# One load of x, turned into columns on VectorE, and a separate buffer for the output rows, in a one-token decoder block

## The chip, the cores and the metric

The kernel runs on one core of a Trainium2 chip. The metric is the device time of the whole kernel in microseconds (us), taken as the median of several executions. An execution counts as slow when it takes over 1.5% longer than the fastest of its kernel.

Engine names in the profile: PE is TensorE's matmuls, PEld its weight loads, DVE is VectorE, ACT is ScalarE, POOL is GpSimd, SP is SyncE. A q behind the name (SPq, ACTq) is the engine's instruction queue, from which DMAs are issued. L143 is line 143 of the kernel. A line number of a helper can stand for many calls.

## The reference

One token passes through an attention layer with a cache of 65,536 positions, then through a gated feed-forward layer. Both have a layer norm before and a residual after.

```python
x = A_x                                   # [1, 1, 1024], bf16
# attention: 32 query heads, 4 kv heads, head size 128
q = layernorm(x) @ wq                     # wq [1024, 4096]
p = softmax(q @ k_cache.T / sqrt(128))    # k_cache, v_cache [1, 4, 65536, 128]
h = x + (p @ v_cache) @ wo                # wo [4096, 1024]
# feed-forward
n = layernorm(h)
out = h + (gelu(n @ w_gate) * (n @ w_up)) @ w_down   # 1024 <-> 3584
```

Everything is read once. The inputs are 173 MB, nearly all of it cache and weights; x and the output are 2 KB each.

## The kernel before

All large tensors pass through one pool of five buffers of 128 x 16384 bf16 (4 MB each). SyncE issues their loads in program order, each as soon as its buffer is free. The first two hold wq, the next three the first parts of k.

x was loaded twice by ScalarE: as columns (128 partitions, 8 elements each) for the layer norm, and as four rows of 256 for the residual, which TensorE adds to the output rows in PSUM.

```python
x_row = lead.tile([4, D // 4], BF16, name="x_row")
x_pc_bf = lead.tile([P, DC], BF16, name="x_pc_bf")          # P = 128, DC = 8
# ...
nc.scalar.dma_start(out=x_pc_bf[:], in_=A_x[0, 0].rearrange("(p c) -> p c", c=DC))
nc.scalar.dma_start(out=x_row[:], in_=A_x[0, 0].rearrange("(g n) -> g n", g=4))
for c0 in range(0, DC, WB):
    wv = load(wq_v[:, c0:c0 + WB, :], "wq_sb")             # two loads of 4 MB on SyncE
# ...
nc.vector.tensor_copy(out=x_pc[:], in_=x_pc_bf[:])
layernorm_cols(x_pc[:], xn_bf[:], "ln1")
# ... xnz (xn in padded columns), q = xn @ wq, k transposes, scores, softmax, values, wo ...
for g in range(4):                                         # the residual
    out_mm(ident_bf[0:4, g:g + 32], lambda g: x_row[:], False, False, groups=[g])
# ... feed-forward, the last matmuls add w_down's product into f_ps ...
o_fin = rows.tile([P, OW], BF16, name="o_fin")             # pool that reuses earlier space
nc.vector.tensor_copy(out=o_fin[0:97, :], in_=f_ps[0:97, :])
nc.sync.dma_start(out=out[0, 0].rearrange("(g n) -> g n", n=OW), in_=o_fin[0:97:32, :])
```

Of the kernel before, what the change touches and what calls it, by code (L numbers as in the profile page):

```python
# [11 lines left out]
BF16 = mybir.dt.bfloat16  # L12
# [5 lines left out]
def kernel(  # L18
# [13 lines left out]
    nc = tc.nc  # L32
    P = 128
    D = A_x.shape[-1]
    Hkv, Sk, Dh = A_k_cache.shape[1], A_k_cache.shape[2], A_k_cache.shape[3]
    HD = A_wq.shape[1]
    Hq = HD // Dh
    rep = Hq // Hkv
    F = B_w_gate.shape[1]
    DC = D // P  # L40
# [19 lines left out]
    lead = ctx.enter_context(tc.tile_pool(name="lead", bufs=1))  # L60
# [3 lines left out]
    sel = lead.tile([P, 32], F32, name="sel")  # L64
    hmask = lead.tile([P, rep], F32, name="hmask")
    x_pc = lead.tile([P, DC], F32, name="x_pc")
    x_row = lead.tile([4, D // 4], BF16, name="x_row")
    ident_bf = lead.tile([P, P], BF16, name="ident_bf")
    x_pc_bf = lead.tile([P, DC], BF16, name="x_pc_bf")
    xn_bf = lead.tile([P, DC], BF16, name="xn_bf")  # L70
    neg_half = lead.tile([P, 1], F32, name="neg_half")
    oT_all = lead.tile([P, Hq], BF16, name="oT_all")
    used = sum(-(-b // 32) * 32 for b in (4 * P, 4 * P, 2 * (W0 + NS * P), 128, 4 * rep, 4 * DC, D // 2, 2 * P,
                                          2 * DC, 2 * DC, 4, 2 * Hq))
    lead.tile([P, (-(used + 128)) % 4096], mybir.dt.uint8, name="lead_pad")
    chpool = ctx.enter_context(tc.tile_pool(name="chpool", bufs=NBUF))
    const = ctx.enter_context(tc.tile_pool(name="const", bufs=1))
    small = ctx.enter_context(tc.tile_pool(name="small", bufs=2))
    ps_m = ctx.enter_context(tc.tile_pool(name="ps_m", bufs=1, space=PSUM))
    actx = ExitStack()  # L80
    qkpool = actx.enter_context(tc.tile_pool(name="qkpool", bufs=2))
# [58 lines left out]
    def mm(out, lhsT, rhs, start, stop, loaded=False, tile_position=None, skip_group_check=False):  # L140
        t = nc.tensor
        if not loaded:
            return pe(t.matmul(out, lhsT=lhsT, rhs=rhs, start=start, stop=stop, tile_position=tile_position,  # L143
                               skip_group_check=skip_group_check))
        op = t.add_instruction(mybir.InstMatmult(  # L145
            name=nc.get_next_instruction_name(), engine=t.engine, start_tensor_calc=start, stop_tensor_calc=stop,
            tile_size=(lhsT.shape[0], lhsT.shape[1]), tile_position=tile_position or (0, 0), ldweights=False,
            bass_skip_group_check=skip_group_check,
            ins=[t.lower_ap(rhs), t.lower_ap(lhsT, for_matmul_weights=True)], outs=[t.lower_ap(out, opt=True)]))
        reuses.add(op.ins.name)  # L150
        return pe(op)
# [11 lines left out]
    wq_v = A_wq.rearrange("(p c) n -> p c n", c=DC)  # L163
    WB = max(1, CW // HD)
    assert HD <= CW and DC % WB == 0
    nc.scalar.dma_start(out=x_pc_bf[:], in_=A_x[0, 0].rearrange("(p c) -> p c", c=DC))
    nc.scalar.dma_start(out=x_row[:], in_=A_x[0, 0].rearrange("(g n) -> g n", g=4))
    wq_tiles = []
    for c0 in range(0, DC, WB):
        wv = load(wq_v[:, c0:c0 + WB, :], "wq_sb")  # L170
# [15 lines left out]
    for bp in range(4):  # L186
        s0 = 64 * (bp // 2) + bp % 2
        nc.vector.tensor_copy(out=esel[:, bp, :, :],
                              in_=ident_bf[:, s0:s0 + 63:2].unsqueeze(1).to_broadcast([P, 4, 32]))

    def layernorm_cols(src_col, dst_bf, tagp):
        s1 = small.tile([P, 1], F32, name=f"{tagp}_s1", tag="ln_s1")
        nc.vector.tensor_reduce(out=s1[:], in_=src_col, axis=AX.X, op=ALU.add)  # L193
        tot = ps_m.tile([P, 1], F32, name=f"{tagp}_tot", tag="misc")
        mm(tot[:], ones_f[:], s1[:], True, True)
        mean = small.tile([P, 1], F32, name=f"{tagp}_mean", tag="ln_mean")
        nc.vector.tensor_scalar(out=mean[:], in0=tot[:], scalar1=1.0 / D, scalar2=None, op0=ALU.mult)
        xc = small.tile([P, DC], F32, name=f"{tagp}_xc", tag="ln_xc")
        nc.vector.tensor_scalar(out=xc[:], in0=src_col, scalar1=mean[:, 0:1], scalar2=None, op0=ALU.subtract)
        sq = small.tile([P, DC], F32, name=f"{tagp}_sq", tag="ln_sq")  # L200
        s2 = small.tile([P, 1], F32, name=f"{tagp}_s2", tag="ln_s2")
        nc.vector.tensor_tensor(out=sq[:], in0=xc[:], in1=xc[:], op=ALU.mult)
        nc.vector.tensor_reduce(out=s2[:], in_=sq[:], axis=AX.X, op=ALU.add)
        tot2 = ps_m.tile([P, 1], F32, name=f"{tagp}_tot2", tag="misc")
        mm(tot2[:], ones_f[:], s2[:], True, True)
        ve = small.tile([P, 1], F32, name=f"{tagp}_ve", tag="ln_ve")
        nc.vector.tensor_scalar(out=ve[:], in0=tot2[:], scalar1=1.0 / D, scalar2=eps, op0=ALU.mult, op1=ALU.add)
        rstd = small.tile([P, 1], F32, name=f"{tagp}_rstd", tag="ln_rstd")
        nc.gpsimd.tensor_tensor(out=rstd[:], in0=ve[:], in1=neg_half[:], op=ALU.pow)
        nc.vector.tensor_scalar(out=dst_bf, in0=xc[:], scalar1=rstd[:, 0:1], scalar2=None, op0=ALU.mult)  # L210

    nc.vector.tensor_copy(out=x_pc[:], in_=x_pc_bf[:])  # L212
    layernorm_cols(x_pc[:], xn_bf[:], "ln1")

    def padded(pool, vec, ncols, name, tag=None):
# [192 lines left out]
    rows = ctx.enter_context(tc.tile_pool(name="rows", bufs=1))  # L408
# [19 lines left out]
    for wc in range(Hq // WN):  # L428
        wv = load(wo_v[:, wc * WN:(wc + 1) * WN, :], "wo_sb")
        for cc in range(WN):  # L430
            c = wc * WN + cc
# [4 lines left out]
    OW = D // 4  # L436
    f_ps = ps_f.tile([P, OW], F32, name="f_ps")

    def out_mm(stat, mov, first, last, groups=range(4)):
        for g in groups:  # L440
            mm(f_ps[32 * g:32 * g + 32, :], stat, mov(g), first, last, tile_position=(0, 32 * g),
               skip_group_check=True)
# [1 line left out]
    assert OW == 32 * DC  # L444
    out_mm(ones_f[:, 0:32], lambda g: at_r[:, g // 2, g % 2 * OW:g % 2 * OW + OW], True, False)
    for g in range(4):
        out_mm(ident_bf[0:4, g:g + 32], lambda g: x_row[:], False, False, groups=[g])
    h_t = rows.tile([P, DC, 32], F32, name="h_t")
    nc.vector.transpose(out=h_t[:].rearrange("p c j -> p (c j)"), in_=f_ps[:].rearrange("p (i c) -> p c i", c=DC))
    hn_bf = const.tile([P, DC], BF16, name="hn_bf")  # L450
# [66 lines left out]
    for sz in sizes:  # L517
        wv = load(wd_v[:, c0:c0 + sz, :], "wd_sb")
        for cc in range(sz):
            c = c0 + cc  # L520
            out_mm(actz[:, c, :], lambda g: wv[:, cc, g * OW:(g + 1) * OW], False, c + 1 == FC)
        c0 += sz
    o_fin = rows.tile([P, OW], BF16, name="o_fin")
    nc.vector.tensor_copy(out=o_fin[0:97, :], in_=f_ps[0:97, :])
    nc.sync.dma_start(out=out[0, 0].rearrange("(g n) -> g n", n=OW), in_=o_fin[0:97:32, :])

# [29 lines left out]
```

## Time and profile before

| | before |
|---|---|
| time at first, median of 3 | 408.83 us |
| span of the profiled execution | 407.1 us |
| busy: PE, DVE, ACT | 73%, 50%, 11% |
| moved by DMA | 173.19 MB, 425 GB/s over the span |

The page of the kernel before cuts the span into 40 slices of 10.2 us. A digit of the DMA row is the busy share of the 16 DMA engines in tenths, 9 standing for 90% or more; the row below it is the rate.

```profile
DMA  9999999999999999999999999999999999999995
GB/s 374 451 412 444 430 425 451 410 451 425 427 448 415 454 417 441 435 412 454 422 443 431 422 445 422 440 435 425 441 422 443 431 422 451 417 432 437 434 416 214
q10 hardware_dynamic: 152, 0.00, 0.0%
```

The DMA engines are busy from the first slice to the last but one. PE is idle for a quarter of the span, and no compute engine is near its limit over the whole span. The Trainium skill, "HBM Reference", section "Specifications (TRN2)", says that a core streaming alone measures about 425 GB/s, bounded by its 16 DMA engines. This trace agrees: 425 GB/s over the span. The third line is the queue of ScalarE: 152 packets, those of the two loads of x and their completions.

The issues of the kernel before (tensor, issuing queue, count, KB each, median us from issue to landing):

```profile
k_sb<-in_A_k_cache_dram SPq DMA_DIRECT2D x16, 4096.0 KB, 32.5
x_pc_bf<-in_A_x_dram ACTq DMA_DIRECT2D x1, 2.0 KB, 13.7
```

A 4 MB tile takes about 10 us to move at this rate but lands 32.5 us after its issue: two to three tiles are waiting ahead of it. That is the reserve of the load stream. The 2 KB of x take 13.7 us.

The timeline of the kernel before at the start and at the end (start, duration, engine, line, operation, count; in brackets the idle time before it and what ended it):

```profile
14.56 0.17 DVE L212 CAST x_pc<-x_pc_bf 128x8 f32<-128x8 bf16 x1 [13.49 <-DMA x_pc_bf<-in_A_x_dram]
18.48 0.18 DVE L218 COPY xnz<-xn_bf 128x8 bf16<-128x8 bf16 x1
25.14 0.69 DVE L229 COPY q_ev<-q_ps 128x512 f32<-128x512 f32 x1 [6.47 <-PE q_ps L145]
31.51 8.89 DVE L272 STREAM_TRANSPOSE k_sb<-k_sb 128x2048 uint32<-128x2048 uint32 x4 [3.74 <-DMA k_sb<-in_A_k_cache_dram]
402.97 1.04 PE L143 MATMUL f_ps<-wd_sb,actz 128*32 128x256 bf16 x12 [0.20 <-DMA wd_sb<-in_B_w_down_dram]
404.06 0.42 DVE L524 CAST o_fin<-f_ps 97x256 bf16<-97x256 f32 x1 [11.85 <-PE f_ps L143]
404.57 0.65 SPq L525 DMA_DIRECT2D out_dram<-o_fin  x1
```

Everything at the start waits for x until 14.56 us, q is ready for eviction at 25.14, but the next user, the first transpose of k, waits for its own load until 31.51. At the end the last weights release the last matmuls at 402.97, then come the cast and the output DMA.

### The profile page before, as it was taken

How to read it: one execution, taken by the hardware profiler on the slowest of the kernel's cores; microseconds unless marked ns; L12 is line 12 of the kernel's file. 1: busy time of each engine (PE TensorE's matmuls, PEld its weight loads, DVE VectorE, ACT ScalarE, POOL GpSimd, SP SyncE). 2: the span in 40 equal slices, each digit the busy share in tenths (PEclk: the TensorE clock that was granted, in tenths of full speed). 3: DMA queues.
4: the chain of work that ended last, by engine and by line, in shares of the span. 5: the costliest groups of instructions: out<-in, count | busy, mean ns of one | idle time of the engine just before them, and what ended most of it. 6: DMA issues, size and time to landing. Idle time of an engine off the chain costs nothing.

```text
span 407.1 us, 2657 instructions
## 1 busy us (share of the span) xinstructions
PE 298.8 (73%) x1481; PEld 64.1 (16%) x713; DVE 202.0 (50%) x183; ACT 44.9 (11%) x67; POOL 7.4 (2%) x17
## 2 busy tenths in 40 slices
PE   0266286879996789799966969998767997714464
PEld 0111011111110111211101111110102111300233
DVE  0218989966573678546464878181853001110110
ACT  1010001050000041000000420000051001000000
POOL 2000000000000000000000000000010000100000
PEclk9996879889999969699978798999887899767865
DMA  9999999999999999999999999999999999999995
GB/s 374 451 412 444 430 425 451 410 451 425 427 448 415 454 417 441 435 412 454 422 443 431 422 445 422 440 435 425 441 422 443 431 422 451 417 432 437 434 416 214
DMA packets 6652, 173.19 MB, mean 425 GB/s; under 512 B 872, under 2 KB 880, under 8 KB 1136
## 3 DMA queue, kind: packets, MB, share of 16 engines
q1 hardware_dynamic: 6488, 173.02, 98.7%
q8 instruction: 8, 0.13, 0.1%
q10 hardware_dynamic: 152, 0.00, 0.0%
q14 instruction: 4, 0.03, 0.0%
HBM read 173.02 MB, written 0.00 MB: 425 GB/s over the span
## 4 chain that ended last, share of the span: by engine, by line
DMA 46%; PE 30%; DVE 18%; ACT 4%; issue 1%; SPq 0%; ACTq 0%; DVEq 0%
DMA k_sb<-in_A_k_cache_dram 32%; DVE k_sb L272 12%; PE acc_ps L145 12%; DMA wg_sb<-in_B_w_gate_dram 9%; PE qk_ps L143 6%; PE qk_ps L145 6%; DMA wd_sb<-in_B_w_down_dram 5%; PE acc_ps L143 4%; DVE mx L293 3%; ACT sc L292 2%; DVE pT L317 1%; ACT pe_r L314 1%; PE o_ps L143 1%; DVE acc_sb L343 1%; ACT acc_sb L345 1%
## 5 line engine op out<-in xcount | busy, mean ns | idle before, releaser
L272 DVE STREAM_TRANSPOSE k_sb<-k_sb 128x2048 uint32<-128x2048 uint32 x64 | 142.1, 2278 | 31.6 <-DMA k_sb<-in_A_k_cache_dram 31.6
L143 PE MATMUL qk_ps<-k_sb,wsel 128*128 128x512 bf16 x256 | 103.7, 405 | 34.7 <-DVE k_sb L272 21.3
L145 PE MATMUL acc_ps<-v_sb,pT 128*128 128x512 bf16 x384 | 114.3, 410 | 0.0
L145 PE MATMUL qk_ps<-k_sb,wsel 128*128 128x512 bf16 x256 | 103.2, 403 | 0.0
L143 PE MATMUL acc_ps<-v_sb,pT 128*128 128x512 bf16 x128 | 52.9, 413 | 0.0
L143 PEld LDWEIGHTS <-wsel 128*128 128x128 bf16 x256 | 26.0, 101 | 138.3 <-issue 118.2
L293 DVE TENSOR_REDUCE mx<-qk_ps 128x1 f32<-128x1024 f32 x16 | 19.5, 1220 | 45.8 <-ACT sc L292 45.7
L292 ACT COPY sc<-qk_ps 128x1024 f32<-128x1024 f32 x16 | 16.2, 1012 | 201.8 <-PE qk_ps L145 201.7
L143 PEld LDWEIGHTS <-pT 128*128 128x128 bf16 x128 | 13.8, 108 | 101.9 <-issue 101.9
L317 DVE STREAM_TRANSPOSE pT<-pe_r 128x1024 bf16<-128x1024 bf16 x16 | 19.0, 1227 | 6.2 <-ACT pe_r L314 6.2
L343 DVE COPY acc_sb<-acc_ps 32x512 f32<-32x512 f32 x8 | 5.4, 671 | 32.2 <-PE acc_ps L145 32.1
L314 ACT ACTIVATE pe_r<-sc,nbias 128x1024 bf16<-128x1024 f32 x16 | 18.2, 1140 | 13.7 <-DVE nbias L309 13.0
L143 PE MATMUL ln_tot<-ln_s,ones_f 128*128 128x1 f32 x8 | 1.9, 311 | 17.6 <-DVE ln_s L193 15.7
L145 PE MATMUL wu_ps<-wu_sb,hnz 128*32 128x512 bf16 x40 | 6.4, 524 | 7.5 <-DMA wu_sb<-in_B_w_up_dram 7.5
L143 PE MATMUL o_ps<-sel,acc_sb 128*128 128x8 f32 x32 | 6.6, 335 | 6.7 <-DVE rl L357 6.3
L345 ACT COPY acc_sb<-acc_ps 32x512 f32<-32x512 f32 x8 | 4.6, 577 | 61.4 <-DVE acc_sb L343 61.4
L229 DVE COPY wg_ev<-wg_ps 128x512 f32<-128x512 f32 x1 | 0.7, 692 | 20.6 <-PE wg_ps L143 20.6
L143 PE MATMUL f_ps<-wd_sb,actz 128*32 128x256 bf16 x112 | 6.9, 415 | 5.4 <-DMA wd_sb<-in_B_w_down_dram 5.3
L143 PE MATMUL wg_ps<-wg_sb,hnz 128*32 128x512 bf16 x32 | 5.3, 488 | 6.7 <-DMA wg_sb<-in_B_w_gate_dram 6.7
L154 PE MATMUL mxT_ps<-ident_f,mx 128*1 128x128 f32 x4 | 1.1, 281 | 10.4 <-DVE mx L298 10.4
L143 PEld LDWEIGHTS o_ps<-sel,acc_sb 128*128 128x128 f32 x32 | 6.3, 293 | 7.0 <-issue 6.0
L212 DVE CAST x_pc<-x_pc_bf 128x8 f32<-128x8 bf16 x1 | 0.2, 171 | 13.5 <-DMA x_pc_bf<-in_A_x_dram 13.5
(100 smaller groups left out, 85.5 us busy)
## 6 DMA issues: line engine op xcount, KB each, us to landing
k_sb<-in_A_k_cache_dram SPq DMA_DIRECT2D x16, 4096.0 KB, 32.5
v_sb<-in_A_v_cache_dram SPq DMA_DIRECT2D x16, 4096.0 KB, 36.8
wq_sb<-in_A_wq_dram SPq DMA_DIRECT2D x2, 4096.0 KB, 16.5
wo_sb<-in_A_wo_dram SPq DMA_DIRECT2D x2, 4096.0 KB, 32.0
wg_sb<-in_B_w_gate_dram SPq DMA_DIRECT2D x2, 3584.0 KB, 33.4
wu_sb<-in_B_w_up_dram SPq DMA_DIRECT2D x2, 3584.0 KB, 33.9
wd_sb<-in_B_w_down_dram SPq DMA_DIRECT2D x1, 3584.0 KB
wd_sb<-in_B_w_down_dram SPq DMA_DIRECT2D x1, 1792.0 KB, 25.4
```

The source lines that it names most:

```text
L143: return pe(t.matmul(out, lhsT=lhsT, rhs=rhs, start=start, stop=stop, tile_position=tile_position, skip_group_check=skip_group_check))
L145: op = t.add_instruction(mybir.InstMatmult(name=nc.get_next_instruction_name(), engine=t.engine, start_tensor_calc=start, stop_tensor_calc ...
L154: pe(nc.tensor.transpose(out=out, in_=in_, identity=identity))
L212: nc.vector.tensor_copy(out=x_pc[:], in_=x_pc_bf[:])
L229: nc.vector.tensor_copy(out=dst, in_=src)
L272: dv(nc.vector.transpose(out=kt[:, c * w:(c + 1) * w], in_=kt[:, c * w:(c + 1) * w]))
L292: ac(nc.scalar.copy(out=sc[:], in_=flat))
L293: dv(nc.vector.tensor_reduce(out=state[("mx", g)][:, li:li + 1], in_=flat, axis=AX.X, op=ALU.max))
L314: ac(nc.scalar.activation(out=pe_r[:], in_=state.pop(("sc", g, li))[:], func=ACT.Exp, bias=nbias[:, 0:1], scale=scale, accum_out=lpart[:, ...
L317: dv(nc.vector.transpose(out=pT[:].rearrange("p m c -> p (m c)"), in_=pe_r[:]))
L343: dv(nc.vector.tensor_copy(out=acc_sb[sl, :], in_=acc[sl, c, :]))
L345: ac(nc.scalar.copy(out=acc_sb[sl, :], in_=acc[sl, c, :]))
```

## The change

x is loaded once, as four rows of 512 bytes on partitions 0, 32, 64 and 96. VectorE's transpose of 32x32 blocks turns them into columns. The intent is to replace a slow load of 128 pieces of 16 bytes by four pieces. The output rows get a buffer of their own, so that the output DMA has fewer engines to wait for. Before it waited for VectorE, ScalarE and GpSimd, because others had used that space; after, for VectorE alone.

```diff
-    x_row = lead.tile([4, D // 4], BF16, name="x_row")
+    x_row = lead.tile([P, D // 4], BF16, name="x_row")
-    x_pc_bf = lead.tile([P, DC], BF16, name="x_pc_bf")
+    x_t = lead.tile([P, DC, 32], BF16, name="x_t")
 ... (the sizes of the padding follow)
+    o_fin = const.tile([P, D // 4], BF16, name="o_fin")
 ...
-    nc.scalar.dma_start(out=x_pc_bf[:], in_=A_x[0, 0].rearrange("(p c) -> p c", c=DC))
-    nc.scalar.dma_start(out=x_row[:], in_=A_x[0, 0].rearrange("(g n) -> g n", g=4))
+    nc.vector.memset(x_row[:], 0.0)
+    nc.scalar.dma_start(out=x_row[0:97:32, :], in_=A_x[0, 0].rearrange("(g n) -> g n", g=4))
 ...
-    nc.vector.tensor_copy(out=x_pc[:], in_=x_pc_bf[:])
+    nc.vector.transpose(out=x_t[:].rearrange("p c j -> p (c j)"), in_=x_row[:].rearrange("p (i c) -> p c i", c=DC))
+    nc.vector.tensor_copy(out=x_pc[:], in_=x_t[:, :, 0])
 ...
-        out_mm(ident_bf[0:4, g:g + 32], lambda g: x_row[:], False, False, groups=[g])
+        out_mm(ident_bf[:, 32 * g:32 * g + 32], lambda g: x_row[:], False, False, groups=[g])
 ...
-    o_fin = rows.tile([P, OW], BF16, name="o_fin")
```

More of the change, by code (lines that the diff above doesn't have):

```diff
@@ L73 @@
     used = sum(-(-b // 32) * 32 for b in (4 * P, 4 * P, 2 * (W0 + NS * P), 128, 4 * rep, 4 * DC, D // 2, 2 * P,
-                                          2 * DC, 2 * DC, 4, 2 * Hq))
+                                          64 * DC, 2 * DC, 4, 2 * Hq))
     lead.tile([P, (-(used + 128)) % 4096], mybir.dt.uint8, name="lead_pad")
@@ L210, in layernorm_cols @@
         nc.vector.tensor_scalar(out=dst_bf, in0=xc[:], scalar1=rstd[:, 0:1], scalar2=None, op0=ALU.mult)
-    nc.vector.tensor_copy(out=x_pc[:], in_=x_pc_bf[:])
+    assert D // 4 == 32 * DC
+    nc.vector.transpose(out=x_t[:].rearrange("p c j -> p (c j)"), in_=x_row[:].rearrange("p (i c) -> p c i", c=DC))
+    nc.vector.tensor_copy(out=x_pc[:], in_=x_t[:, :, 0])
     layernorm_cols(x_pc[:], xn_bf[:], "ln1")
```

## The prediction

> **What bounds the kernel now.** The page's first part has PE busy 73% of the 407.1 us span, DVE 50%, ACT 11%; the DMA row of the slices is at 90% or more everywhere but in the last. The table of stretches gives a DMA share of 0.95 to 1.05 and 421 to 442 GB/s from 30 us to 390 us. The Trainium skill, "HBM Reference", section Access, says that a core streaming alone measures about 425 GB/s, bounded by its 16 DMA engines; this trace agrees (425 over the span). The load queue runs ahead: median issue to landing is 32.5 us for a 4 MB k tile that takes about 10 us to move, so two to three tiles are always queued. What the compute engines do in between hardly matters. Three things set the time: the start (about 1.4 us), the bytes, and the tail after the last weights (last matmuls 402.97 to 404.06, output cast 0.42 us, output DMA issued at 404.57, end at 407.1).
>
> **What the change does.**
> 1. Head. Two loads of x become one. The 128x8 load, 16 bytes a partition, takes 13.7 us to land, and VectorE waits 13.5 us for it. The Trainium skill, "DMA: Bandwidth & Descriptors", section "Queues, rings and completion order", says that a DMA engine takes turns between queues packet by packet; this trace fits: 8 pieces plus a completion on each engine at 13.7 us is about 1.5 us a turn beside the big wq packets. Four pieces of 512 bytes on four engines need about two turns: I estimate landing 2 to 5 us after an issue near 1.2 us (it now waits for a memset of about 0.1 us).
> 2. VectorE gains that memset and a 128x256 bf16 transpose: estimated 0.3 to 0.45 us, from 1227 ns for 128x1024 bf16 and 0.45 us for 128x256 f32. The chain from x to xnz (14.56 to 18.72 us) becomes 4.5 us long but starts 10 us sooner: xnz near 8 to 10 us. The q matmuls then wait for wq, whose halves land at about 12 and 21 us, and end near 23.5 to 25 us, against 25.1. Their consumer, the first k transpose, waits for its own load until 31.5 us in both. Value on the critical path: 0.
> 3. The x packets that go: ScalarE's queue has 152 packets and shows 0.0% of 16 engines' span, so under 0.2 us for each engine. Expect at most 0.1 us.
> 4. The residual matmuls (4 of 0.28 us at 355.7 us) get 128 rows instead of 4: same 256 columns, same time, and weights are queued far ahead there.
> 5. The output DMA waits for VectorE alone, no longer for ScalarE and GpSimd too. Those had long been done, and it was issued 0.09 us after the cast: at most 0.05 us.
>
> **Prediction.** 408.6 us, against 408.83: range 407.8 to 409.4. Faster by over 2%: 0.01; within 2%: 0.98; slower by over 2%: 0.01.
>
> **What would show it.** Right: x lands by about 6 us; VectorE's 13.5 us wait for x falls below 5 us; PE's wait before the q matmuls is put down to wq; the first k transpose still starts near 31.5 us; DMA rate in every slice as before; the tail within 0.2 us of before. Wrong on step 1: x lands after 10 us. Wrong on steps 3 or 5: the last weights land over 0.3 us earlier or later, or the tail changes by more.
>
> **What would make it wrong.** A DMA stream that runs at another rate because the small packets go or because some buffers move by 512 bytes; a gap in the load queue that different timing opens.

## The result, and the profile after

| | before | after |
|---|---|---|
| time, median (6 runs each) | 408.82 us | 408.74 us |
| lowest to highest | 408.75 to 409.3 us | 408.64 to 408.93 us |
| span of the profiled execution | 407.1 us | 407.0 us |

The ratio is 0.9996, with a 95% interval of 0.9983 to 1.0008. Ratios here are the mean time of one kernel's fast runs over that of the other's of the same rounds, so not quite the ratio of the medians. The two kernels can't be told apart by time.

The slices and ScalarE's queue of the changed kernel:

```profile
DMA  9999999999999999999999999999999999999995
GB/s 364 461 412 451 423 419 457 410 454 422 414 461 415 441 430 415 461 415 444 427 419 457 415 448 425 420 454 415 448 426 432 440 419 444 424 429 442 426 421 220
q10 hardware_dynamic: 8, 0.00, 0.0%
```

The queue of ScalarE fell from 152 packets to 8: four pieces and four completions. This agrees with the Trainium skill, "DMA: Bandwidth & Descriptors", section "Why a DMA increments its semaphore by 16 and not by 1", which says that a load issued from ScalarE spreads over as many engines, up to 16, as divide the slowest dimension of both sides, here four, and that each of them adds one completion. The DMA row did not change. The first two slices together moved as fast as before (364 + 461 = 825 against 374 + 451 = 825).

The timeline of the changed kernel at the places shown of before:

```profile
1.09 1.08 ACTq L168 DMA_DIRECT2D x_row<-in_A_x_dram  x1
7.19 0.63 DVE L214 STREAM_TRANSPOSE x_t<-x_row 128x256 bf16<-128x256 bf16 x1 [5.98 <-DMA x_row<-in_A_x_dram]
11.75 0.18 DVE L221 COPY xnz<-xn_bf 128x8 bf16<-128x8 bf16 x1
21.75 0.62 PE L144 MATMUL q_ps<-wq_sb,xnz 128*32 128x512 bf16 x4 [6.24 <-DMA wq_sb<-in_A_wq_dram]
25.40 0.69 DVE L232 COPY q_ev<-q_ps 128x512 f32<-128x512 f32 x1 [13.47 <-PE q_ps L146]
31.45 2.31 DVE L275 STREAM_TRANSPOSE k_sb<-k_sb 128x2048 uint32<-128x2048 uint32 x1 [3.41 <-DMA k_sb<-in_A_k_cache_dram]
402.92 1.02 PE L144 MATMUL f_ps<-wd_sb,actz 128*32 128x256 bf16 x12 [0.17 <-DMA wd_sb<-in_B_w_down_dram]
403.99 0.42 DVE L526 CAST o_fin<-f_ps 97x256 bf16<-97x256 f32 x1 [11.82 <-PE f_ps L144]
404.44 0.66 SPq L527 DMA_DIRECT2D out_dram<-o_fin  x1
```

x can be used at 7.19 us instead of 14.56, and xnz is ready 6.7 us sooner. That gain ends at the next two waits. The second half of wq holds TensorE until 21.75 us, and q is no sooner ready than before: 25.40 us against 25.14. The 0.26 us between these two are within the scatter of this stage: in the run `out_only` below, whose start is that of the kernel before, q was ready at 23.93 us. The first transpose of k starts at its load's landing as before. At the end, the last weights come within 0.05 us of before, and the output DMA follows the cast after 0.03 instead of 0.09 us.

So the change did its local work, and the total did not move. Why that is so can be tested: theory A says that only the load stream, its start and its tail set the time. The rivals: B, two effects cancel; C, the packets that went are worth time of their own in the DMA engines; D, the head of the compute is on the path, and something ate its gain.

### The profile page after: what moved, and what is told of

Its sections match the earlier page's. It is cut to its first block, busy times and chain, and to the rows that moved or that the text cites. A ratio compares the mean times of both kernels' runs of the same rounds, so it can differ in the third digit from the quotient of the medians.

```text
span 407.0 us, 2658 instructions
## 1 busy us (share of the span) xinstructions
PE 299.3 (74%) x1481; PEld 62.8 (15%) x713; DVE 202.6 (50%) x185; ACT 44.9 (11%) x67; POOL 7.4 (2%) x17
## 4 chain that ended last, share of the span: by engine, by line
DMA 46%; PE 30%; DVE 18%; ACT 4%; issue 2%; SPq 0%; ACTq 0%; DVEq 0%
DMA k_sb<-in_A_k_cache_dram 32%; DVE k_sb L275 12%; PE acc_ps L146 12%; DMA wg_sb<-in_B_w_gate_dram 8%; PE qk_ps L144 6%; PE qk_ps L146 6%; DMA wd_sb<-in_B_w_down_dram 5%; PE acc_ps L144 4%; DVE mx L296 2%; ACT sc L295 2%; DVE pT L320 1%; ACT pe_r L317 1%; PE o_ps L144 1%; DVE acc_sb L346 1%; ACT acc_sb L348 1%
## 5 line engine op out<-in xcount | busy, mean ns | idle before, releaser
L144 PE MATMUL qk_ps<-k_sb,wsel 128*128 128x512 bf16 x256 | 103.9, 406 | 36.3 <-DVE k_sb L275 23.8
L146 PE MATMUL acc_ps<-v_sb,pT 128*128 128x512 bf16 x384 | 112.6, 405 | 0.0
L144 PE MATMUL acc_ps<-v_sb,pT 128*128 128x512 bf16 x128 | 52.0, 406 | 0.0
L144 PE MATMUL q_ps<-wq_sb,xnz 128*32 128x512 bf16 x32 | 5.2, 626 | 8.0 <-DMA wq_sb<-in_A_wq_dram 8.0
L144 PE MATMUL wg_ps<-wg_sb,hnz 128*32 128x512 bf16 x32 | 6.5, 598 | 5.3 <-DMA wg_sb<-in_B_w_gate_dram 5.3
L144 PE MATMUL o_ps<-sel,acc_sb 128*128 128x8 f32 x32 | 5.2, 290 | 6.7 <-DVE rl L360 5.9
```

The costliest lines, as they stand in the source:

```text
L144: return pe(t.matmul(out, lhsT=lhsT, rhs=rhs, start=start, stop=stop, tile_position=tile_position, skip_group_check=skip_group_check))
L146: op = t.add_instruction(mybir.InstMatmult(name=nc.get_next_instruction_name(), engine=t.engine, start_tensor_calc=start, stop_tensor_calc ...
```

## The experiments

There were twelve runs. All of them gave outputs within the tolerance, also the two that are wrong, so that check says little about the part that was broken; probably the attention part is small beside the residual in this data. In the diffs below the base is the changed kernel unless it says otherwise. The ratios and the gains of time are against the kernel before, timed in the same rounds (408.75 to 408.96 us). The places in the timelines are compared with the trace of the changed kernel. The quoted texts are the expectations before each run; where two stand together, they follow the order of the kernels named.

### Each part of the change alone

The first kernel (`out_only`) is the one before with only `o_fin` moved to its own buffer; the second (`x_only`) is the changed kernel with `o_fin` put back.

```diff
 (first, from the kernel before)
+    o_fin = const.tile([P, D // 4], BF16, name="o_fin")
-    o_fin = rows.tile([P, OW], BF16, name="o_fin")
 (second, from the changed kernel)
-    o_fin = const.tile([P, D // 4], BF16, name="o_fin")
+    o_fin = rows.tile([P, OW], BF16, name="o_fin")
```

> Only the output row moves; x is loaded as in the kernel before. Theory A (the load stream from the first to the last weight sets the time, with compute far behind in need): 408.7 us, within 0.1% of before; the output DMA is issued 0.03 to 0.05 us sooner after the cast. Theory B (the two parts of the change have opposite effects that cancel): this run and the next differ from before in opposite directions by more than 0.2%.

> Only the load of x changes; the output row stays in the shared region. Theory A: 408.7 us, within 0.1% of before, although VectorE waits about 6 us for x instead of 13.5. Theory B: more than 0.2% from before, with the sign opposite to the run of the output row alone. Theory C (the 144 small packets that go are worth time in the DMA engines): at least 0.3 us faster than before.

Measured: the output row alone 408.91 us, ratio 1.0001 (0.9984 to 1.0018); the load of x alone 408.86 us, ratio 0.9999 (0.9984 to 1.0014). The timeline's end with the output row alone:

```profile
404.11 0.42 DVE L524 CAST o_fin<-f_ps 97x256 bf16<-97x256 f32 x1 [11.80 <-PE f_ps L144]
404.56 0.65 SPq L525 DMA_DIRECT2D out_dram<-o_fin  x1
```

And with the load of x alone:

```profile
404.03 0.42 DVE L526 CAST o_fin<-f_ps 97x256 bf16<-97x256 f32 x1 [11.77 <-PE f_ps L143]
404.54 0.66 SPq L527 DMA_DIRECT2D out_dram<-o_fin  x1
```

The gap between the cast's end and the issue is 0.03 us where the row has its own buffer and 0.09 us where it has not. This part of the change is real and worth about 0.06 us. Theory B falls as far as it was told: neither part moves the time by 0.2% (0.8 us) either way. Theory C's forecast for the load of x, at least 0.3 us faster than before, did not come (408.86 us in both), but the interval of about 0.6 us either way doesn't exclude it.

### The head made late on purpose

Dead memsets on VectorE are put ahead of the transpose of x, 24 in one kernel and 48 in the other.

```diff
+    busy = scpool.tile([P, 2 * 512], F32, name="busy", tag="sc0")
+    for _ in range(24):          # 48 in the second
+        dv(nc.vector.memset(busy[:], 0.0))
-    nc.vector.transpose(out=x_t ...)
+    dv(nc.vector.transpose(out=x_t ...))
```

> The changed kernel with 24 dead memsets of 128x1024 on VectorE (estimated 1.1 us each, about 27 us in all) ahead of the transpose of x: the head of the compute is made later than it ever was. Theory A: the load queue holds about 50 us of work from the start, so it stays full and the time stays at 408.7 us, at most 409.5. Rival D (the head is on the path, and the 6 us that x gained were eaten by something else): the time grows by a good part of 27 us, to over 420 us.

> As before with 48 dead memsets, about 54 us. Theory A: the buffers of wq come free only near 70 us, but the five loads in flight are done near 51 us, so the DMA row shows a gap of some 15 to 20 us there and the time grows by about as much, to 424 to 432 us. If the slack is larger than I think, less; rival D: the difference to the run with 24 memsets is the full 27 us.

Measured: 408.71 us with 24 memsets (ratio 0.9995, 0.998 to 1.001), and 442.92 us with 48 (ratio 1.0837). The timeline with 24:

```profile
34.56 0.18 DVE L224 COPY xnz<-xn_bf 128x8 bf16<-128x8 bf16 x1
38.24 2.06 SPq L161 DMA_DIRECT2D k_sb<-in_A_k_cache_dram  x2
```

A dead memset took 0.91 us and the next began 0.28 us after it, so 24 of them make 29 us and 48 make 57 us. The timeline with 48, where VectorE also put eight transposes of k (2.3 us each) between the steps of the layer norm, so that the first buffer of wq came free near 82 us, not near 70 as I had reckoned:

```profile
77.72 0.19 DVE L224 COPY xnz<-xn_bf 128x8 bf16<-128x8 bf16 x1
81.69 2.06 SPq L161 DMA_DIRECT2D k_sb<-in_A_k_cache_dram  x2
```

And the slices with 48, which are 11 us wide in this longer span:

```profile
DMA  9999500599999999999999999999999999999995
GB/s 381 428 428 440 227 0 0 199 444 449 428 428 383 429 434 440 443 429 431 431 428 429 431 434 440 441 426 431 434 428 435 429 431 437 432 429 434 434 419 233
```

This is the main finding. xnz 22.8 us later than in the changed kernel (34.56 against 11.75) costs nothing that the runs can show (at most 0.1%, or 0.4 us, by the interval), so being 6.7 us sooner can gain nothing; rival D falls. The slack has an end: the fourth k load needs the first wq buffer. With 24 memsets it is issued at 38 us, while loads are still under way. With 48 it is issued at 81.69 us; the five tiles of the start were done near 49 us, the DMA engines then idle for about 33 us, and the time grows by 34 us. My 15 to 20 us for it was too low mostly because of the extra lateness just told, 11.7 us of the missing 14 to 19.

### The three exposed places: bytes, start, tail

First, the second half of wo is never loaded, and its matmuls take the first half again (wrong):

```diff
-        wv = load(wo_v[:, wc * WN:(wc + 1) * WN, :], "wo_sb")
+        if wc == 0:
+            wv = load(wo_v[:, wc * WN:(wc + 1) * WN, :], "wo_sb")
```

> The changed kernel with the second half of the output weights never loaded; its matmuls use the first half again, so all compute stays and the result is wrong on purpose. 4.19 MB of 173 MB go. Theory A: at 431 GB/s that is 9.7 us, so 399.0 us (398.5 to 399.8). If compute set the time: 408.7 us.

Measured: 399.34 us, ratio 0.977 (0.9755 to 0.9785), 9.4 us less than both kernels for 4.19 MB, with all the compute kept; the last matmuls start at 393.36 us instead of 402.92. The bytes set the time.

Second, four dead loads of x lead on SyncE:

```diff
+    for i in range(4):
+        nc.sync.dma_start(out=x_dead[:, i, :], in_=A_x[0, 0].rearrange("(p c) -> p c", c=DC))
     wq_tiles = []
```

> The changed kernel with four dead 128x8 loads of x first on SyncE, ahead of the first wq load: the stream of weights starts about 1.9 us later (issues of about 0.35 us and the start barrier ahead of it). Theory A: the start of the stream is exposed in full, 410.2 to 411.0 us. If the head were hidden: 408.7 us. The first dead load, on an empty queue, shows the landing time without turns beside wq: about 2 us.

Measured: 411.1 us, ratio 1.0058 (1.0043 to 1.0073). The timeline and the issues of this kernel:

```profile
2.13 0.91 SPq L161 DMA_DIRECT2D wq_sb<-in_A_wq_dram  x2
3.05 0.63 DVE L217 STREAM_TRANSPOSE x_t<-x_row 128x256 bf16<-128x256 bf16 x1 [1.84 <-DMA x_row<-in_A_x_dram]
405.00 1.04 PE L144 MATMUL f_ps<-wd_sb,actz 128*32 128x256 bf16 x12 [0.19 <-DMA wd_sb<-in_B_w_down_dram]
x_dead<-in_A_x_dram SPq DMA_DIRECT2D x4, 2.0 KB, 1.6
```

The first wq load is issued at 2.13 us instead of 0.00, the last matmuls start 2.08 us later (405.00 against 402.92), and the time grows by 2.35 us (0.1 us above my range; its difference from the other two numbers is within the scatter of single executions). x is in use at 3.05 us here, sooner than in any other run, and the kernel is slower all the same. What counts at the start is when the weights begin to flow, not when x arrives.

Third, seven dependent copies stand between the cast and the output DMA:

```diff
     nc.vector.tensor_copy(out=o_fin[0:97, :], in_=f_ps[0:97, :])
+    for _ in range(3):
+        nc.vector.tensor_copy(out=o_mid[0:97, :], in_=o_fin[0:97, :])
+        nc.vector.tensor_copy(out=o_fin[0:97, :], in_=o_mid[0:97, :])
+    nc.vector.tensor_copy(out=o_fin2[0:97, :], in_=o_fin[0:97, :])
```

> The changed kernel with seven dependent VectorE copies of the output rows (97x256 bf16, estimated 0.2 to 0.3 us each with the gap) between the cast and the output DMA. Theory A: the tail after the last weights is exposed in full: 410.1 to 410.8 us. If the tail were hidden behind something: 408.7 us.

Measured: 410.58 us, ratio 1.0043 (1.0027 to 1.006). The first copy and the output DMA in the timeline:

```profile
404.68 0.23 DVE L530 COPY o_mid<-o_fin 97x256 bf16<-97x256 bf16 x1
406.51 0.66 SPq L533 DMA_DIRECT2D out_dram<-o_fin  x1
```

A copy takes 0.23 us and the next starts 0.26 us after the start of the one before; seven make 1.83 us, and the time grew by 1.83 us (410.58 against 408.75). That the two agree to the last digit is luck, as the interval allows 1.1 to 2.5 us. The tail is exposed in full. So the 0.06 us of the output buffer do lie on the path; they are just too small to see in the time.

### Are the small packets free?

A dead load behind the load of x brings back small packets, at four times and at twice the dose that the change took away.

```diff
-    nc.scalar.dma_start(out=x_row[0:97:32, :], ...)
+    ac(nc.scalar.dma_start(out=x_row[0:97:32, :], ...))
+    x_dead = const.tile([P, 4, DC], BF16, name="x_dead")     # [P, 2, DC] in the second
+    ac(nc.scalar.dma_start(out=x_dead[:], in_=A_x[0, 0].rearrange("(p c) -> p c", c=DC).unsqueeze(1).to_broadcast([P, 4, DC])))
```

> The changed kernel with one dead load on ScalarE's queue that reads x four times in 16-byte pieces (512 data packets, 32 on each engine), behind the load of x: the small packets that the change took away, four times over. Theory A with a packet cost of at most 0.1 us: time within 0.3% of 408.7, at most 1 us more. Theory C: over 1.2 us slower. Turn model: 33 turns of 1.1 us and 3.8 us fixed (fitted from 9 turns in 13.7 us and 2 turns in 6.0 us) give a landing about 40 us after the issue; with 1.5 us a turn and no fixed part it would be 50 us, and if landing did not depend on the turns, under 15 us.

> Half the dose of the run with four dead reads of x: 256 small packets, 16 on each engine, behind the load of x. The larger dose cost 1.2 to 1.3 us. If each small packet has a fixed price (1.25 us over 33 on an engine, 38 ns), this one costs 17 times 38 ns: 0.6 to 0.7 us more than the changed kernel, about 409.4 us, and the one small load that the change took away was worth about 0.3 us, more than the at most 0.1 us of the prediction. If the larger dose hit something that the small load did not, at most 0.2 us: 408.7 to 408.9 us. Landing by the turn model: 19 turns of 1.1 us and 4 us, about 25 us after the issue.

Measured: 410.03 us with the dose of four (ratio 1.0033, 1.0018 to 1.0048), 409.36 us with the dose of two (ratio 1.0012, 0.9998 to 1.0026; one of its five runs was at 408.96). The last matmuls' lines with four:

```profile
404.20 1.00 PE L144 MATMUL f_ps<-wd_sb,actz 128*32 128x256 bf16 x12 [0.21 <-DMA wd_sb<-in_B_w_down_dram]
x_dead<-in_A_x_dram ACTq DMA_DIRECT2D x1, 8.0 KB, 41.3
```

And with two:

```profile
403.56 0.99 PE L144 MATMUL f_ps<-wd_sb,actz 128*32 128x256 bf16 x12 [0.20 <-DMA wd_sb<-in_B_w_down_dram]
DMA to landing us min/median/max: 24.7/24.7/24.7
```

Against 402.92 us in the changed kernel the last weights come 1.28 us later for 33 packets on each engine, and 0.64 us later for 17: 39 and 38 ns a packet. The larger dose is clear of the noise, the smaller by its time alone is not. These are single traces, and such traces scatter: in six kernels that load the same bytes with the new load of x and without a gap (`after`, `x_only`, 24 memsets, 16 and 31 dead matmuls, seven copies) the last matmuls start at 402.78 to 403.14 us. So the two doses fit a price in proportion to the number, but the second price could be off by about a third. By it the 9 packets an engine that the change took away would be worth 0.34 us. Between the kernels before and after, however, the last weights moved by 0.05 us only, and the means of the times differ by 0.04%, or 0.16 us, with an interval that contains both 0 and 0.34 us. The other runs lean against 0.34 us: the two traces with the old load of x, 402.97 and 403.02 us (`before`, `out_only`), lie within the range of those six, and the first five of the six were on average 0.1 us faster than the kernel before, the gain of the output buffer included. Whether the small load had its price in the kernel before stays open; theory C is not refuted, only bounded.

The landing times fit turns. On the busiest DMA engines there were 2 packets of x in the changed kernel (landed 6.1 us after the issue began), 9 before (13.7 us), 19 with the dose of two (24.7 us, with the two of x ahead) and 35 with four (41.3 us). The steps between these are 1.09, 1.10 and 1.04 us a packet, over a fixed part of about 4 us. A landing can slip by one such turn: the same load of x in four pieces was in use at 8.24 us with the dose of two and at 8.17 us in the last run below, against 7.19 us. The Trainium skill, "DMA: Bandwidth & Descriptors", section "Queues, rings and completion order", says that an engine takes turns between queues packet by packet and that a packet typically holds about 9 to 17 descriptors. The turns agree. Here each 16-byte piece behaves as a packet of its own: the page counts 152 packets for 128 + 4 pieces and 16 + 4 completions. With nothing queued ahead, the same load landed in 1.6 us (the run with four leading loads), so most of the fixed part comes from what is queued ahead. That last step is inferred, and so is that a packet of the profile is what the page calls a packet; the landing times, one turn for each piece, speak for it.

### Why the second half of q was slow: TensorE's clock

In the changed kernel TensorE runs half of q at 12.1 us, idles 6.2 us, and runs the other half. Dead matmuls fill the gap, 16 in one kernel and 31 in the other.

```diff
+        if c == DC // 2:
+            for i in range(16):          # 31 in the second
+                mm(qt_ps[0:32, 0, :, :].rearrange("p b n -> p (b n)"), xnz[:, 0, :], wq_tiles[0][:, 0:512], True, True)
         wide_mm(q_banks, xnz[:, c, :], ...)
```

> The changed kernel with 16 dead matmuls of 32x512 between the two halves of the q matmuls, about 6.8 us, which fill TensorE's idle time while it waits for the second wq half. My reading of the changed trace is that the second half of q ran at 634 ns a matmul because TensorE had been idle for 6 us. If so, the second half now runs at 377 to 420 ns and the q matmuls end near 23.5 us instead of 25.4. Theory A: the time stays at 408.7 us (within 0.1%) all the same, because the first k transpose waits for its load until 31.5 us.

> The run with 16 dead matmuls left 3.0 us of idle time, and the second half of q ran slow again. With 31 dead matmuls (16 took 3.6 us) the gap of 6.6 us is filled to within 0.5 us. If idle time before it is what makes the second half slow, its matmuls now follow each other every 0.21 us instead of 0.43 and the q matmuls end near 23.7 us instead of 25.4. The time stays at 408.7 us in any case.

Measured: 408.8 us with 16 (ratio 0.9997, 0.998 to 1.0013) and 408.9 us with 31 (ratio 1.0, 0.9987 to 1.0014). The timeline with 16:

```profile
15.14 3.62 PE L144 MATMUL qt_ps<-wq_sb,xnz 128*32 128x512 bf16 x16
21.76 0.62 PE L144 MATMUL q_ps<-wq_sb,xnz 128*32 128x512 bf16 x4 [3.00 <-DMA wq_sb<-in_A_wq_dram]
25.30 0.69 DVE L232 COPY q_ev<-q_ps 128x512 f32<-128x512 f32 x1 [13.40 <-PE q_ps L146]
```

And with 31:

```profile
15.16 6.85 PE L144 MATMUL qt_ps<-wq_sb,xnz 128*32 128x512 bf16 x31
21.81 0.42 PE L144 MATMUL q_ps<-wq_sb,xnz 128*32 128x512 bf16 x4
23.79 0.69 DVE L232 COPY q_ev<-q_ps 128x512 f32<-128x512 f32 x1 [11.71 <-PE q_ps L146]
31.48 2.31 DVE L278 STREAM_TRANSPOSE k_sb<-k_sb 128x2048 uint32<-128x2048 uint32 x1 [5.05 <-DMA k_sb<-in_A_k_cache_dram]
```

Sixteen dead matmuls ran faster than I had reckoned, because the clock had just risen, and left 3.0 us idle; the second half was slow again. With the gap filled, the second half starts at about the same time and is ready 1.6 us sooner (23.79 against 25.40). Its groups of matmuls follow each other every 0.21 us, against 0.43 us. The granted clock of the profile says the same: from 22 to 23.8 us it is 0.50 of full speed with 16 dead matmuls and 1.00 with 31. With 16 it fell at about 21.6 us, 2.9 us after the end of the last dead matmul; in the changed kernel at about 18.6 us, 3.1 us after the end of the first half of q. So it was the idle time that made it slow. (Before its first change that clock reads 1.00 even at 12 to 14 us, where the matmuls go at the slow pace of 0.43 us; there the pace is to be believed.) The Trainium skill, "TensorE: Matmul & The Clock Gate", section "What's actually happening", says that TensorE runs at half its clock by default and after an idle window of about 3.4 us, and at full clock after sustained work of about 3.4 us. The runs agree in kind: half the pace after the idle time, 0.43 us against 0.21. In number an idle time of 3.0 us was enough here. The time did not follow q: the first transpose of k still waits until 31.48 us.

### The transpose of x

The transpose reads its row in order instead of in steps of eight elements. Its output is wrong, which doesn't matter for the time.

```diff
-    nc.vector.transpose(out=x_t[:]..., in_=x_row[:].rearrange("p (i c) -> p c i", c=DC))
+    nc.vector.transpose(out=x_t[:]..., in_=x_row[:])
```

> The changed kernel with the transpose of x reading its row in order instead of in steps of 8 elements; the result is wrong on purpose. One look at one instruction: if the stepped read is what made it 626 ns instead of my estimate of 300 to 450, it takes 300 to 400 ns here; if not, 626 ns again. No change of the time is expected.

Measured: 408.53 us in one timing (state unknown), and 445 ns instead of 626 for the instruction; both had waited for x. The stepped read costs 181 ns here; the rest was my estimate's error, since even the plain form is at the upper end of it. The 626 ns are not the stepped form's time everywhere: in the two kernels with dead memsets, where it followed another VectorE instruction without a wait, the same instruction took 494 ns. Why was not tested.

## Why the prediction was right, point by point

- **What bounds the kernel:** right, and now shown. 4.19 MB less are 9.4 us less; 2.13 us later wq is 2.35 us more; 1.83 us more tail is 1.83 us more; xnz 22.8 us later is nothing. Only the head was made late; that the compute in the middle has slack too rests on the full DMA row and was not tested. The time came out 0.14 us above the point forecast, inside the range and within 2%. That hit is weak evidence alone, as no change at all would have been inside too, and the gain of 0.2 us in the forecast is neither shown nor excluded.
- **Step 1, x lands sooner:** right in kind, wrong in size. I expected 2 to 5 us after the issue; it took 6.1 us. I had put all of the 13.7 us into nine turns of 1.5 us; the runs show turns of 1.04 to 1.10 us and a fixed part of about 4 us. So x was in use at 7.2 us, not by about 6, and VectorE's wait fell to 6.0 us, not below 5 us.
- **Step 2, the chain to q:** value on the path 0, right. The sizes were off: the transpose took 0.63 us against 0.3 to 0.45, xnz came at 11.9 us (end of its copy) against 8 to 10, and q was ready at 25.40 us against 23.5 to 25. I had left out that the idle time between the halves of wq makes TensorE slow again; with the gap filled q was ready at 23.79 us, in the range of the prediction. PE's wait was put down to wq, and the first k transpose started at 31.45 us, both as said.
- **Step 3, the packets:** not settled. The estimate of at most 0.1 us fits the trace pair (0.05 us) and the other runs' traces, but not the price measured by adding packets (38 to 39 ns each, 0.34 us for nine). The times can't decide between them.
- **Step 4, the residual matmuls:** right. The four matmuls took 273 ns with 128 rows, 278 ns with 4.
- **Step 5, the output DMA:** right in size: 0.06 us less between cast and issue, just over the forecast of at most 0.05.

No version came out of this that beats both kernels by an amount the runs could show.

## What to carry to other kernels

Before you make something earlier, see what its consumer waits for next: here a gain of 7 us met a wait for wq and then a wait for k. Where the DMA row is full from end to end and loads are issued tiles ahead, as here, look for gains in the bytes, the first issue and the tail. Making a stage late on purpose is a cheap test of its slack: 23 us of lateness for nothing says that 7 us of gain are worth nothing, and a second, larger dose shows where the slack ends.

## What the Trainium skill lacked or had wrong

- "DMA: Bandwidth & Descriptors" gives no landing time for a small load beside a busy queue. Here a load of 2 KB landed in 1.6 us with nothing ahead, in 6.1 us as 4 pieces and in 13.7 us as 128 pieces of 16 bytes beside 4 MB loads: about 4 us plus 1.04 to 1.10 us for each packet on an engine.
- The same page gives a packet as typically about 9 to 17 descriptors; in this trace each 16-byte piece counted as a packet (152 for the two loads of x with completions), and each cost a turn of 1.04 to 1.10 us.
- The same page names overheads of small packets, but no price for one in a full stream of other loads. Here 33 and 17 more on each engine delayed the last weights by 1.28 and 0.64 us, 38 to 39 ns each.
- "TensorE: Matmul & The Clock Gate" says that the clock falls after an idle window of about 3.4 us and rises after about as long of work, and also that the window runs free, so that the count of slow matmuls varies. Here 3.0 us of idle time were enough, and the speed-up came between 2.5 us (the run with 16 dead matmuls, 12.11 to 14.63) and 5.5 us (before, 18.72 to 24.24) after the first matmul of a stretch of q. `out_only`, with the same start as before, sped up after 2.5 us (18.84 to 21.38). The free-running window may explain the spread, but no run here tests that.
- "VectorE: DVE Perf Modes" gives a time for a transpose, but neither it nor another page gives in numbers what a stepped read costs it on VectorE: 626 ns against 445 ns in order, for 128x256 bf16, both after a wait.
